# The last down projection of a SwiGLU layer, computed one Strassen product at a time

## The chip, the cores and the metric

The kernel runs on one core of one Trainium2 chip. The metric is the time of one execution on the device in microseconds (us). Of several runs the median is given.

## The reference, cut to what matters

S = 2048 tokens, D = 1024, F = 3584, all in bf16.

```
xn  = layernorm(x)
s   = linear_attention(xn, wqkv, wo)
h   = silu(xn @ w_gate) * (xn @ w_up)        # 2048 x 3584
B   = h @ w_down                             # 2048 x 1024: the down projection
out = x + s * silu(B)
```

## The kernel before, in words

The attention part comes first and writes `s` to a scratch array in HBM (`s_dram`). The feed-forward part follows in two passes of 1024 tokens (`passes`, the upper half of the tokens first). In a pass the gate and up products come as 28 units ("keys": 14 slices of 256 columns, gate and up), and their results make `h`, which stays in SBUF as one tile `hT` of [128, 28, 1024]. Then `emit_down` computes the down projection of the pass.

All these products are done by a seven-product scheme of the Strassen kind (Winograd's form). For the down projection the 1024 tokens of `h` are split into an upper and a lower half (`TB` = 512 tokens each), its 3584 columns into even and odd blocks of 128, and w_down into 2 x 2 blocks. With A for h and B for w_down there are sums S1 = A21 + A22, S2 = S1 - A11, S3 = A11 - A21, S4 = A12 - S2 of h and four sums T1 to T4 of w_down. The latter were formed in the first pass and lie in HBM in packs: `wd_drams[j]` holds for two of the 14 blocks an "a" part (T1, T2, T3, B11) and a "b" part (B21, B22, T4). A product is a sum over 14 blocks, so 14 matmuls of 128x512 for each of the four token tile pairs; with seven products and four pairs there are 392.

`emit_down` goes over the token tile pairs in two halves. Phase a (`step_a`) computes four products at once for one pair, into four PSUM banks: for each block k the products with B11, T2, T3 and T1. Phase b (`step_b`) computes the other three. The sums S1 to S3 of h are made unit by unit by `emit_hs` (L1064 to L1067: four operations on [128, 512], S4 in place of A21) into a ring of six buffers, just ahead of phase a, mostly on VectorE. `evac_a` and `evac_b` add the products up on VectorE and apply the silu on ScalarE. The last pair of the last pass is done by `finish`, product after product, with the last one split into 384 and 128 columns.

`fin` (L1096 to L1098) ends an output block: two operations on VectorE, y * s and + x, and a store on SP's queue. The pieces of x and s for it (`io`) are loaded by `io_load` on the same queue, five to eight ahead, in the order of the list `fq`.

The order on TensorE (PE), VectorE (DVE), ScalarE (ACT) and GpSimd (POOL) is written out by hand (`manual_schedule`); a scheduler places the transfers in SP's queue. Weight buffers come from a ring of eight (`wgu`, 1 MB each), filled in the order of `w_seq` by `load_w_to`. PSUM is held by two pools: `pps` has four tiles of one bank, `ppd` has two tiles of two banks each. The waits between engines are set by the framework, from what each instruction reads and writes.

In the gate and up stage `emit_b` adds a second round of products to the tile `zw` of `ppd`, whose two halves were read by two VectorE operations after the first round:

```python
            nc.vector.scalar_tensor_tensor(out=s3[:], in0=zw[:, 0, :], scalar=rc, in1=s2[:],
                                           op0=ALU.mult, op1=ALU.add)                        # L968
            nc.vector.scalar_tensor_tensor(out=dst, in0=zw[:, 1, :], scalar=rc_of(key),
                                           in1=s3[:], op0=ALU.mult, op1=ALU.add)             # L981
            mb = prod(x_[:], lambda k: w[:, HK + k, 0:P], lambda k: x1[:, HK + k, :], False)
            prod(zw[:, 0, :], lambda k: T4[:, k, :], lambda k: a22[:, k, :], False)
            prod(zw[:, 1, :], lambda k: w[:, HK + k, P:2 * P], lambda k: S4[:, k, :], False)
```

Lines that the text names: L512, L515, L517 and L528 are transposes, copies and products of the first stage of the kernel; L939 is the matmul of the gate and up products; L1006, L1008, L1020 write `h`; L1124 is the matmul of the down projection; L1163 to L1171 and L1183 to L1192 are its evacuation; L234 loads the packs of w_down.

Of the kernel before, what the change touches and what calls it, by code (L numbers as in the profile page):

```python
# [9 lines left out]
ACT = mybir.ActivationFunctionType  # L10
# [11 lines left out]
def kernel(  # L22
# [164 lines left out]
    NPASS = NB // 2  # L187
    passes = list(range(NPASS - 1, -1, -1))
    NWA = NFG // 2
    w_seq = []  # L190
    for p in passes:
        for fg in range(NFG):
            w_seq.append((p, "g", fg))
            w_seq.append((p, "u", fg))
        for kd in ("a", "b"):
            for j in range(NWA):
                w_seq.append((p, kd, j))
# [10 lines left out]
    def wd_q(t):  # L208
        return t[:].rearrange("p h a b -> p (h a b)").rearrange("p (q n) -> p q n", n=D)
# [15 lines left out]
    def load_w():  # L225
        key = w_seq[w_next[0]]
        w_next[0] += 1
        if key in w_tiles:
            return
        p, kind, k = key  # L230
        t = w_slot()
        if kind in ("a", "b"):
            src = wd_drams[k][0 if kind == "a" else 1]
            nc.sync.dma_start(out=t[:].rearrange("p h a b -> p (h a b)")[:, 0:2 * WDN[kind]],  # L234
                              in_=src[:].rearrange("p k q n -> p (k q n)"))
        elif key[1:] in pk_drams:
            gate([nc.sync.dma_start(out=t[:], in_=pk_drams[key[1:]][:])], first_gate[0], sync=True)
        else:
            load_gu(t, kind, k, first_gate[0])
            raw_keys.add(key)  # L240
        w_tiles[key] = t
# [684 lines left out]
    with ExitStack() as p3:  # L926
# [7 lines left out]
        def k2(shape, dt, name):  # L934
            return kp.tile(shape, dt, name=name, tag="k2")
# [117 lines left out]
        def emit_hs(h, hf, m, eng):  # L1053
            r = (NWA * hf + m + 5) % 6
            if r >= 3:
                st = m4.tile([P, HK, TB], F16, name="hs", tag="m4")
            else:
                st = sp.tile([P, HK, TB], F16, name="S%d" % r, tag="S%d" % r)
            sv = st[:].rearrange("p a b -> p (a b)").rearrange("p (q k t) -> p q k t", q=4, k=2)
            hv = h[:, 4 * m:4 * m + 4, :].rearrange("p (k a) t -> p k a t", a=2)  # L1060
            t1, t2 = slice(hf * HT, (hf + 1) * HT), slice(TB + hf * HT, TB + (hf + 1) * HT)
            a11, a12, a21, a22 = hv[:, :, 0, t1], hv[:, :, 1, t1], hv[:, :, 0, t2], hv[:, :, 1, t2]
            S1, S2, S3 = [sv[:, q] for q in range(3)]
            eng.tensor_tensor(out=S1, in0=a21, in1=a22, op=ALU.add)  # L1064
            eng.tensor_tensor(out=S2, in0=S1, in1=a11, op=ALU.subtract)
            eng.tensor_tensor(out=S3, in0=a11, in1=a21, op=ALU.subtract)
            eng.tensor_tensor(out=a21.bitcast(F16), in0=a12, in1=S2, op=ALU.subtract)  # L1067
            s_ring[(hf, m)] = (S1, S2, S3)
# [3 lines left out]

        fq = []
        for p in passes:
            fq += [(p, t + TPB, 1) for t in range(TPB)]
            for hf in (1, 0):
                for t in (2 * hf, 2 * hf + 1):
                    fq += [(p, t + TPB, 0), (p, t, 1), (p, t, 0)]
# [23 lines left out]
        def emit_down(p, h, base, last, more_S, next_S):  # L1102
# [151 lines left out]
            for hf in (1, 0):  # L1254
# [25 lines left out]
                else:  # L1280
                    for f in fins2:
                        f()

        base = 0
        for pi, p in enumerate(passes):
            h = hp.tile([P, FC, TB2], BF16, name="hT", tag="hT")
            keys = [(p, kd, fg) for fg in range(NFG) for kd in ("g", "u")]
            n = len(keys)
            first = pi == 0
            last_pass = pi == NPASS - 1  # L1290

            if first:
                first_gate[0] = marks[("S", NB - 1, 0)]

            def raw(j):
                return 0 <= j < n and keys[j] in raw_keys

            def pipe(j):
                if raw(j):
                    emit_st0(keys[j], w_tiles[keys[j]])  # L1300

            def pipe1(k, i):
                if raw(k):
                    emit_st1(keys[k], grp[keys[i + 1]][4][:, 0:1])

            def pipe2(j):
                if raw(j):
                    t = w_tiles[keys[j]]
                    emit_st2(keys[j], t, later=j == n - 1)
                    emit_lk(keys[j][2])  # L1310
                    if j < n - 1:
                        emit_T(keys[j], t)
                    raw_keys.discard(keys[j])

            wd_live = {}

            def wd_pipe(i):
                if (i - 3) % 3 == 0 and i // 3 - 1 in wd_live:
                    key, t = wd_live[i // 3 - 1]
                    w = raw_view(key, t)  # L1320
                    nc.scalar.activation(out=w, in_=w, func=ACT.Copy, scale=cs_all[:, kcol(key):kcol(key) + 1])
                if (i - 1) % 3 == 0 and (i - 1) // 3 in wd_live:
                    emit_st0(*wd_live[(i - 1) // 3])

            def wd_pipe1(i):
                if (i - 2) % 3 == 0 and (i - 2) // 3 in wd_live:
                    emit_st1(wd_live[(i - 2) // 3][0], grp[keys[i + 1]][4][:, 1:2])

            def wd_pipe2(i):
                m, r = divmod(i + 1, 3)  # L1330
                if r == 1 and m - 1 in wd_live:
                    emit_T(*wd_live[m - 1])
                elif r == 0:
                    if m - 1 in wd_live:
                        emit_st2(*wd_live[m - 1], later=True)
                    if NWE + m < NFG:
                        t = w_slot()
                        load_wd(t, NWE + m)
                        wd_live[m] = ((p, "w", NWE + m), t)

            def more_S(m):
                if first:
                    scale_h(h, 2 * m, nc.scalar)
                    scale_h(h, 2 * m + 1, nc.vector)
                emit_hs(h, 0, m, nc.vector)

            def next_S(m):
                emit_hs(h, 1, m, nc.vector)

            def tail():  # L1350
                emit_hs(h, 0, 2, nc.vector)
                if first:
                    scale_h(h, 7, nc.scalar)
                emit_hs(h, 0, 3, nc.vector)

            na0 = 6 if first else 8
            load_w_to(base + na0)
            if first:
                wd_pipe2(-1)
            emit_a(keys[0])  # L1360
            emit_c22(keys[0])
            first_gate[0] = None
            for i in range(n):
                load_w_to(base + i + (na0 if i < n - 7 else 8 if i > n - 6 or not first else 7))
                if i + 1 < n:
                    emit_a(keys[i + 1])
                    emit_c22(keys[i + 1])
                for j in (range(5) if i == 0 else (i + 4,) if i != n - 6 else ()):
                    pipe(j)
                if first:  # L1370
                    wd_pipe(i)
                    for k in {n - 4: (0,), n - 3: (2, 4), n - 2: (5, 6)}.get(i, ()):
                        scale_h(h, k, nc.scalar)
                mb = emit_b(keys[i])
                if first and i in range(n - 6, n - 1):
                    io_load(mb)
                pipe1(i + (4 if i == n - 5 else 3), i)
                if first:
                    wd_pipe1(i)
                if i == n - 2:  # L1380
                    emit_hs(h, 0, 0, nc.gpsimd)
                if i == n - 1:
                    emit_hs(h, 0, 1, nc.vector)
                emit_evac(keys[i], h, tail if i == n - 1 else None)
                pipe2(i + (4 if i == n - 5 else 3))
                if first:
                    wd_pipe2(i)
                    if i == 5:
                        emit_lk(0)
                    if i == n - 5:  # L1390
                        emit_lam()
                    elif i == n - 4:
                        emit_sc(keys[-1], w_tiles[keys[-1]])
                        emit_T(keys[-1], w_tiles[keys[-1]])
                        scale_h(h, 1, nc.vector)
                    elif i == n - 3:
                        scale_h(h, 3, nc.vector)
                if deferred:
                    deferred.pop(0)()
            base += n  # L1400
            emit_down(p, h, base, last_pass, more_S, next_S)
            base += 2 * NWA
    man.close()

# [30 lines left out]
```

## Time and profile before

| | |
|---|---|
| median of 3 runs | 758.12 us (758.07 to 758.3) |
| span of the profiled execution | 756.7 us |
| what lies outside the span, by the median | 1.4 us |
| PE busy | 746.6 us, 99% of the span |
| DVE busy | 558.5 us, 74% |
| ACT busy | 376.3 us, 50% |
| POOL busy | 278.4 us, 37% |
| down projection of the last pass, first to last matmul | 667.97 to 752.77 us |

The page gives one profiled execution: the span from its first to its last instruction, and the busy time of each engine in it. It gives no other time of that execution; what lies outside is the difference to the median of the timed runs. A matmul's shown duration is longer than the interval to the next, since matmuls are pipelined: 128x512 is shown with 379 ns, and the next starts 216 ns after it.

### The profile page before, as it was taken

The page shows a single profiled execution, that of the slowest core. Times are in us where ns is not written, and L with a number is a line of the kernel's source. Part 1 is how long each engine was busy: PE and PEld are TensorE (multiplying, and loading weights), DVE is VectorE, ACT ScalarE, POOL GpSimd, SP SyncE. Part 2 cuts the span into 40 slices and gives each one's busy share as a digit, 9 for nine tenths or more (in the row PEclk, how much of TensorE's full clock was granted, in tenths as well). Part 3 has the DMA queues.
Part 4 walks back from the last instruction along what each step waited for, and adds up shares of the span by engine and source line. Part 5 has one row for each costly group of instructions (what it writes and reads, how often), then busy time and mean ns, then how long its engine had stood idle before and what let it go on. Part 6 is the DMA issues. An engine that isn't in the chain of part 4 may idle for free.

```text
span 756.7 us, 10426 instructions
## 1 busy us (share of the span) xinstructions
PE 746.6 (99%) x3662; PEld 349.0 (46%) x3731; DVE 558.5 (74%) x1031; ACT 376.3 (50%) x526; POOL 278.4 (37%) x352
## 2 busy tenths in 40 slices
PE   8999999999999999999999999999999999999997
PEld 4544544454454444444444444444444444444443
DVE  6687787896697788888889775368676777787335
ACT  5677776889956565666659311132322223211122
POOL 2444799998540276868585000100000000200000
PEclk9999999999999999999999999999999999999999
DMA  9968799879679668878799236398644445530824
GB/s 316 295 149 146 223 334 300 302 137 307 201 180 298 229 217 292 309 268 312 278 329 408 86 121 239 124 377 321 229 174 167 167 168 173 180 133 15 283 83 135
DMA packets 105845, 170.30 MB, mean 225 GB/s; under 512 B 34816, under 2 KB 82176, under 8 KB 95168
## 3 DMA queue, kind: packets, MB, share of 16 engines
q1 hardware_dynamic: 100144, 144.99, 59.3%
q0 software_dynamic: 4208, 22.15, 7.5%
q10 hardware_dynamic: 1440, 2.49, 0.9%
q8 instruction: 29, 0.48, 0.3%
q14 instruction: 24, 0.20, 0.1%
HBM read 111.67 MB, written 50.59 MB: 214 GB/s over the span
## 4 chain that ended last, share of the span: by engine, by line
PE 97%; DVE 1%; ACT 1%; issue 1%; ACTq 0%; DVEq 0%
PE zw L939 26%; PE kv_ps L528 15%; PE xb L939 13%; PE dzw L1124 12%; PE yb L939 6%; PE q_ps L183 6%; PE dx L1124 6%; PE dy L1124 3%; PE fx L790 3%; PE s_ps L748 2%; PE kvz L550 1%; PE nd L717 1%; PE df L1124 1%; PE warm_ps L564 1%; DVE w_sb L283 0%
## 5 line engine op out<-in xcount | busy, mean ns | idle before, releaser
L939 PEld LDWEIGHTS <-w_sb 128*128 128x128 f16 (+1 forms) x1568 | 152.1, 98 | 182.7
L939 PE MATMUL xb<-xnT,w_sb 128*128 128x512 bf16 x420 | 113.3, 379 | 1.5
L528 PE MATMUL kv_ps<-wkv_sb,xnT 128*128 128x512 bf16 x499 | 112.9, 379 | 1.1 <-DVE xnT L515 0.3
L939 PE MATMUL zw<-xnT,w_sb 128*128 128x512 bf16 x448 | 105.8, 379 | 0.0
L939 PE MATMUL zw<-S,w_sb 128*128 128x512 f16 x448 | 105.8, 379 | 0.0
L295 POOL TENSOR_TENSOR w_sb<-w_sb 128x512 f16<-128x512 bf16 x42 | 50.2, 1195 | 95.7 <-DVE w_sb L283 51.3
L260 ACT ACTIVATE w_sb<-w_sb 128x2048 bf16<-128x2048 bf16 x42 | 79.9, 1902 | 4.4 <-DMA w_sb<-in_B_w_up_dram 4.4
L1124 PE MATMUL dx<-w_sb,hT 128*128 128x512 bf16 x202 | 76.6, 379 | 0.3
L528 PEld LDWEIGHTS <-xnT 128*128 128x128 bf16 x512 | 48.4, 98 | 55.9 <-ACT xnT L517 0.8
L1124 PEld LDWEIGHTS <-hT 128*128 128x128 bf16 (+1 forms) x462 | 44.7, 98 | 52.4
L183 PE MATMUL q_ps<-xnT,wq_sb 128*128 128x512 bf16 x249 | 58.0, 379 | 0.4
L1015 ACT ACTIVATE sg<-cg 128x1024 bf16<-128x1024 f32 x28 | 29.6, 1057 | 57.4 <-DVE cg L1008 57.4
L939 PE MATMUL yb<-S,w_sb 128*128 128x512 f16 x224 | 57.4, 378 | 0.1
L1124 PE MATMUL dzw<-w_sb,hT 128*128 128x512 f16 (+1 forms) x190 | 57.0, 379 | 0.0
L1008 DVE SCALAR_TENSOR_TENSOR cg<-zw,rc_all,s 128x1024 f32<-128x1024 f32 x28 | 35.9, 1284 | 25.5 <-PE zw L939 13.8
L967 DVE SCALAR_TENSOR_TENSOR s<-yb,rc_all,s 128x512 f32<-128x512 f32 x42 | 31.5, 749 | 28.1 <-ACT s L966 28.1
L296 POOL TENSOR_TENSOR w_sb<-w_sb 128x512 f16<-128x512 bf16 x42 | 50.5, 1201 | 3.3
L1064 POOL TENSOR_TENSOR hs<-hT 128x512 f16<-128x512 bf16 x2 | 2.5, 1250 | 132.6 <-ACT sg L1015 132.6
L298 POOL TENSOR_TENSOR w_sb<-w_sb 128x512 f16<-128x512 bf16 x42 | 50.2, 1196 | 0.0
L297 POOL TENSOR_TENSOR w_sb<-w_sb 128x512 f16<-128x512 bf16 x42 | 50.2, 1195 | 0.0
L1098 POOL DMA_DIRECT2D out_dram<-io x16 | 8.7, 542 | 101.9 <-DVE io L1097 101.6
L966 ACT ACTIVATE s<-xb,rcl 128x512 f32<-128x512 f32 x14 | 9.6, 687 | 65.3 <-PE xb L939 65.3
(179 smaller groups left out, 1187.4 us busy)
## 6 DMA issues: line engine op xcount, KB each, us to landing
w_sb<-pk_g SPq DMA_DIRECT2D x27, 1024.0 KB, 6.3
pk_g<-w_sb SPq DMA_DIRECT2D x14, 1024.0 KB, 5.0
w_sb<-wd SPq DMA_DIRECT2D x14, 1024.0 KB, 6.0
w_sb<-pk_u SPq DMA_DIRECT2D x14, 1024.0 KB, 5.0
pk_u<-w_sb POOLq DMA_DIRECT2D x13, 1024.0 KB, 5.3
w_sb<-wd SPq DMA_DIRECT2D x14, 768.0 KB, 4.8
w_sb<-in_B_w_gate_dram SPq DMA_DIRECT2D x14, 512.0 KB, 6.7
w_sb<-in_B_w_down_dram SPq DMA_DIRECT2D x28, 256.0 KB, 4.9
```

The source lines that it names most:

```text
L183: nc.tensor.matmul(q_ps[:], lhsT=wq_sb[:, dc, g * P:(g + 1) * P], rhs=xn_ap(dc, btok), start=(dc == 0), stop=(dc == DC - 1))
L260: nc.scalar.activation(out=junk, in_=raw_view(key, t), func=ACT.Square, accum_out=asum[:])
L295: nc.gpsimd.tensor_tensor(out=T1, in0=b12, in1=b11, op=ALU.subtract)
L296: nc.gpsimd.tensor_tensor(out=T2, in0=b22, in1=T1, op=ALU.subtract)
L297: nc.gpsimd.tensor_tensor(out=T3, in0=b22, in1=b12, op=ALU.subtract)
L298: nc.gpsimd.tensor_tensor(out=T4, in0=b21, in1=T2, op=ALU.subtract)
L528: mm = nc.tensor.matmul(kv_ps[:], lhsT=xn_ap(dc, tok), rhs=wkv_sb[:, dc, c * CW:(c + 1) * CW], start=(dc == 0), stop=(dc == DC - 1))
L939: mm = nc.tensor.matmul(out, lhsT=lhs(k), rhs=rhs(k), start=(first and k == 0), stop=(k == HK - 1), skip_group_check=True)
L967: nc.vector.scalar_tensor_tensor(out=s2[:], in0=y_[:], scalar=rc, in1=s1[:], op0=ALU.mult, op1=ALU.add)
L1008: nc.vector.scalar_tensor_tensor(out=d12, in0=zw[:], scalar=rc, in1=s2[:, None, :].to_broadcast([P, 2, TB]), op0=ALU.mult, op1=ALU.add)
L1015: nc.scalar.activation(out=sg[:, 1:3, :], in_=cf[:], func=ACT.Silu)
L1124: nc.tensor.matmul(out, lhsT=lhs, rhs=rhs, start=first, stop=lastk, skip_group_check=True)
```

## The change

In the last pass `emit_down_m` takes the place of `emit_down`. It goes over the seven products in the order 1, 2, 7, 6, 5, 4, 3 (product 1 is A11 B11, 2 is A12 B21, 3 is S4 B22, 4 is A22 T4, 5, 6 and 7 are S1 T1, S2 T2, S3 T3), and within each over the four token tile pairs (`TPB` = 4), 14 matmuls each. The loads take one product's slice out of all seven packs, in two halves per product, so a half comes as four transfers with rows of 1 KB instead of one with rows of 6 or 8 KB. The sums of h are made for all blocks at once: S3 in two buffers of the pool `xnp`, S1, S2 and S4 in place of A21, A11 and A12. The banks of a product come from `pps` (products 1 and 2, 6, 4) or from `ppd`, two token tiles to one tile (products 7, 5 and 3). Partial sums are kept in `kA` and `kB`. The order of the outputs in `fq` follows. The sums that the last unit of the gate and up stage made ahead (`emit_hs`, `tail`) are left out in the last pass.

```diff
+    M_ORDER = (1, 2, 7, 6, 5, 4, 3)
+    M_PACK = {1: ("a", 3), 5: ("a", 0), 6: ("a", 1), 7: ("a", 2), 2: ("b", 0), 3: ("b", 1), 4: ("b", 2)}
...
+        if p == passes[-1]:
+            w_seq += [(p, "m", (M, hf)) for M in M_ORDER for hf in range(2)]
+            continue
...
+        elif kind == "m":
+            (M, hf), (kd, q) = k, M_PACK[k[0]]
+            v = wd_q(t).rearrange("p q n -> p (q n)").rearrange("p (k n) -> p k n", n=CW)
+            for j in range(NWA):
+                k0, k1 = max(2 * j, NWA * hf), min(2 * j + 2, NWA * (hf + 1))
+                if k0 < k1:
+                    nc.sync.dma_start(out=v[:, k0 - NWA * hf:k1 - NWA * hf],
+                                      in_=wd_drams[j][0 if kd == "a" else 1][:, k0 - 2 * j:k1 - 2 * j, q])
...
+            if p == passes[-1]:
+                fq += [(p, t + dt, cc) for dt, cc in ((0, 0), (TPB, 1), (TPB, 0), (0, 1)) for t in range(TPB)]
+                continue
...
+        def emit_down_m(p, h, base):
+            hv = h[:].rearrange("p (k a) t -> p k a t", a=2)
+            A11, A12 = hv[:, :, 0, 0:TB], hv[:, :, 1, 0:TB]
+            A21, A22 = hv[:, :, 0, TB:TB2], hv[:, :, 1, TB:TB2]
+            S1, S2, S4 = [v.bitcast(F16) for v in (A21, A11, A12)]
+            s3_ = [xnp.tile([P, NWA, TB], F16, name="S3h", tag="xn8") for _ in range(2)]
+            EV = (nc.vector, nc.vector, nc.sync)
...
+            def sums(out, a, b_, op, part=slice(0, NFG)):
+                for k in range(part.start, part.stop, 2):
+                    nc.vector.tensor_tensor(out=out(k), in0=a[:, k:k + 2], in1=b_[:, k:k + 2], op=op)
...
+            def s3_sums():
+                for k in range(NFG):
+                    nc.vector.tensor_tensor(out=S3(k), in0=A11[:, k], in1=A21[:, k], op=ALU.subtract)
...
+            def mm(M, t, k, out, first, cols=slice(0, CW)):
+                nc.tensor.matmul(out, lhsT=lhs_of(M)(k)[:, t * P:(t + 1) * P], rhs=w_of(M, k)[:, cols],
+                                 start=first and k == 0, stop=k == NFG - 1, skip_group_check=True)
+
+            def prod_t(M, t, out, first):
+                for k in range(NFG):
+                    mm(M, t, k, out, first)
+
+            def s_banks():
+                return [pps.tile([P, CW], FP32, name="dx", tag="s")[:] for _ in range(TPB)]
+
+            def d_banks():
+                v = [ppd.tile([P, 2, CW], FP32, name="dz", tag="d") for _ in range(TPB // 2)]
+                return [v[t // 2][:, t % 2] for t in range(TPB)]
...
+            def load(n):
+                load_w_to(base + 2 * n + NPK)
+
+            load(0)
+            E = s_banks()
+            KA = kept("kA")
+            for t0 in (0, 2):
+                for k in range(NFG):
+                    for t in (t0, t0 + 1):
+                        mm(1, t, k, E[t], True)
+                if t0 == 0:
+                    s3_sums()
+                for t in (t0, t0 + 1):
+                    nc.scalar.copy(out=KA[t], in_=E[t])
+            load(1)
+            sums(at(S1), A21, A22, ALU.add)
+            g = []
+            for t in range(TPB):
+                prod_t(2, t, E[t], False)
+                g.append(silu(E[t], "g11"))
+                if t == 0:
+                    sums(at(S2), S1, A11, ALU.subtract)
+                else:
+                    fin(p, t - 1, 0, g[t - 1], *EV)
+            load(2)
+            fin(p, TPB - 1, 0, g[-1], *EV)
+            O = d_banks()
+            KB = kept("kB")
+            for t in range(TPB):
+                prod_t(7, t, O[t], True)
+                add(KB[t], O[t], KA[t])
+                if t == 0:
+                    sums(at(S4), A12, S2, ALU.subtract)
+            load(3)
+            E = s_banks()
+            for t in range(TPB):
+                prod_t(6, t, E[t], True)
+                add(KB[t], E[t], KB[t])
+                add(KA[t], E[t], KA[t])
+            load(4)
+
+            def out_of(M, bank, K, t, row, cc, pre):
+                c = k2([P, CW], FP32, "c%d" % M)[:]
+                add(c, bank, K)
+                g_ = silu(c, "g%d" % M)
+                if pre is not None:
+                    fin(*pre, *EV)
+                return (p, row, cc, g_)
+
+            pre = None
+            O = d_banks()
+            for t in range(TPB):
+                prod_t(5, t, O[t], True)
+                pre = out_of(5, O[t], KB[t], t, t + TPB, 1, pre)
+            add(KA[-1], O[-1], KA[-1])
+            E = s_banks()
+            for t in range(TPB):
+                prod_t(4, t, E[t], True)
+                pre = out_of(4, E[t], KB[t], t, t + TPB, 0, pre)
+            fin(*pre, *EV)
...
+            for t in range(TPB - 1):
+                prod_t(3, t, O[t], False)
+                pre = out_of(3, O[t], KA[t], t, t, 1, pre)
+            fin(*pre, *EV)
...
-            emit_down(p, h, base, last_pass, more_S, next_S)
+            if last_pass:
+                emit_down_m(p, h, base)
+            else:
+                emit_down(p, h, base, last_pass, more_S, next_S)
```

The end of `emit_down_m`, left out here, computes the last tile of product 3 in two banks of `pps`, 384 and 128 columns, as `finish` does it with its last product.

More of the change, by code (lines that the diff above doesn't have):

```diff
@@ L1282, in emit_down, with S3, lhs_of, at @@
                         f()
+        def emit_down_m(p, h, base):
[5 more added lines that the diff above has]
+            EV = (nc.vector, nc.vector, nc.sync)
+            def S3(k):
+                return s3_[k // NWA][:, k % NWA]
+            def lhs_of(M):
+                if M == 7:
+                    return S3
+                v = {1: A11, 2: A12, 3: S4, 4: A22, 5: S1, 6: S2}[M]
+                return lambda k: v[:, k]
+            def sums(out, a, b_, op, part=slice(0, NFG)):
+                for k in range(part.start, part.stop, 2):
+                    nc.vector.tensor_tensor(out=out(k), in0=a[:, k:k + 2], in1=b_[:, k:k + 2], op=op)
+            def at(v):
+                return lambda k: v[:, k:k + 2]
+            def s3_sums():
+                for k in range(NFG):
+                    nc.vector.tensor_tensor(out=S3(k), in0=A11[:, k], in1=A21[:, k], op=ALU.subtract)
+            def w_of(M, k):
+                t = w_tiles[(p, "m", (M, k // NWA))]
+                v = wd_q(t).rearrange("p q n -> p (q n)").rearrange("p (k n) -> p k n", n=CW)[:, k % NWA]
+                return v.bitcast(F16) if M >= 4 else v
+            def mm(M, t, k, out, first, cols=slice(0, CW)):
[9 more added lines that the diff above has]
+                return [v[t // 2][:, t % 2] for t in range(TPB)]
+            def kept(nm):
+                v = [m4.tile([P, 2, CW], FP32, name=nm, tag="m4") for _ in range(TPB // 2)]
+                return [v[t // 2][:, t % 2] for t in range(TPB)]
+            def add(out, a, b_):
+                nc.vector.tensor_tensor(out=out, in0=a, in1=b_, op=ALU.add)
+            def silu(c, nm):
+                g_ = k2([P, CW], BF16, nm)[:]
+                nc.scalar.activation(out=g_, in_=c, func=ACT.Silu, scale=rch)
+                return g_
+            def load(n):
[55 more added lines that the diff above has]
+            fin(*pre, *EV)
+            hs_ = [slice(0, 3 * CW // 4), slice(3 * CW // 4, CW)]
+            ps = [pps.tile([P, CW], FP32, name="df%d" % i, tag="s")[:] for i in range(2)]
+            for i in range(2):
+                nc.scalar.copy(out=ps[i][:, 0:hs_[i].stop - hs_[i].start], in_=KA[-1][:, hs_[i]])
+            pre = None
+            for t in range(TPB - 1):
+                prod_t(3, t, O[t], False)
+                pre = out_of(3, O[t], KA[t], t, t, 1, pre)
+            fin(*pre, *EV)
+            t = TPB - 1
+            g12 = k2([P, CW], BF16, "g12")[:]
+            for i, cs in enumerate(hs_):
+                o_ = ps[i][:, 0:cs.stop - cs.start]
+                for k in range(NFG):
+                    mm(3, t, k, o_, False, cs)
+                nc.scalar.activation(out=g12[:, cs], in_=o_, func=ACT.Silu, scale=rch)
+                fin(p, t, 1, g12, *EV, cols=cs)
@@ L1379 @@
                     wd_pipe1(i)
[L1380 to L1384, printed above, removed]
+                if not last_pass:
+                    if i == n - 2:
+                        emit_hs(h, 0, 0, nc.gpsimd)
+                    if i == n - 1:
+                        emit_hs(h, 0, 1, nc.vector)
+                emit_evac(keys[i], h, tail if i == n - 1 and not last_pass else None)
                 pipe2(i + (4 if i == n - 5 else 3))
```

## The prediction

> **What bounds the kernel now.** I read the page first (busy times, the chain that ended last), then the last 90 us in stretches of 10 us, then TensorE's (PE's) timeline there, and at last the few places early in the kernel where PE really waits for another engine.
>
> ```profile
> PE 746.6 (99%) x3662; PEld 349.0 (46%) x3731; DVE 558.5 (74%) x1031; ACT 376.3 (50%) x526; POOL 278.4 (37%) x352
> PE 97%; DVE 1%; ACT 1%; issue 1%; ACTq 0%; DVEq 0%
> ```
>
> PE is busy for 99% of the span and carries 97% of the chain. So the kernel is one queue of matmuls, and a change can help only by taking matmuls out, by closing a gap, or by shortening what follows the last matmul. It can hurt by opening a gap.
>
> ```profile
> 680.00:690.00 10.00, 9.95 (x48) 4.52 (x47) 5.20 (x11) 1.31 (x2) 0.00 (x0) 1.00 0.01 2
> 690.00:700.00 10.00, 10.00 (x47) 4.56 (x47) 9.41 (x23) 1.31 (x2) 0.00 (x0) 1.00 0.08 26
> 740.00:750.00 10.00, 9.95 (x48) 4.61 (x47) 5.98 (x12) 2.84 (x5) 0.00 (x0) 1.00 0.57 181
> 750.00:757.00 7.00, 2.77 (x27) 1.84 (x24) 3.13 (x9) 1.89 (x4) 0.00 (x0) 0.86 0.19 59
> ```
>
> ```profile
> 667.97 0.38 PE L1124 MATMUL dx<-w_sb,hT 128*128 128x512 bf16 x1
> 743.51 3.18 PE L1124 MATMUL dz<-w_sb,hT 128*128 128x512 f16 x14
> 746.53 6.24 PE L1124 MATMUL df<-w_sb,hT 128*128 128x512 bf16 x41
> ```
>
> First the stretches, whose columns are the length, then busy time of PE, weight load, VectorE (DVE), ScalarE (ACT), GpSimd (POOL), the granted clock, DMA share and GB/s; then PE's timeline. The stage that is changed runs from 667.97 to 752.77 (746.53 + 6.24). Before the last group there are 26 x 14 = 364 full matmuls in 746.53 - 667.97 = 78.56 us, 0.2158 us from start to start: no gap at all. The 14 that go into one bank in a row (dz) take 746.53 - 743.51 = 3.02 us, again 0.216 each, so repeating a bank costs nothing. DVE, not PE, has the slack. Behind the last matmul lie 756.7 - 752.77 = 3.9 us, and outside the span 758.12 - 756.7 = 1.4 us.
>
> **The change, part by part.** In the built order both programs have the same matmuls: seven products x 4 token tiles x 14, with the last one split 384 + 128. PE's work is 84.8 us before and after; nothing is won there.
>
> *Sums of h.* Away go 14 units of four 128x512 sums, 52 on DVE at 0.42 (21.9 us) and 4 on POOL at 1.15. Instead DVE gets 14 of 128x512 (5.9 us) and 21 of 128x1024. A 128x1024 sum of 16-bit data isn't in the trace; the 128x512 form takes 0.425, the 128x1536 form (L1020) 0.954, which puts it at 0.69 on the straight line and at 0.85 as two of the small. I take 0.69 (14.5 us in all) and keep 0.85 for the range. They run beside PE: DVE ends the last piece of h near 671.2; S3 ends near 677, S1 near 682, S2 near 686.5. They are needed at product 7 (692), 5 (716 and later) and 6 (704). The first product needs only A11, whose last piece (L1006) ends at 669.1 and is read as k = 13 at 667.97 + 26 x 0.216 = 673.6. So cost nothing; without that cover DVE would stand 4 to 5 us in PE's way for each sum.
>
> *Weights.* 14 loads become 56 on SP's queue (a product's slice q comes out of seven buffers, in rows of 1 KB). SP needs 0.32 to 0.5 us for an issue, so 8 x 0.43 = 3.4 us for each 12 us product. Queued behind them are the output stores and the x/s pieces for `fin`. The halves of products 1, 2, 7 and the first of 6 are issued in the seven 6 us units before 668, those of 5, 4 and 3 three products ahead of their use. The wqkv loads at the start have 1 KB rows too:
>
> ```profile
> 5.00:10.00 5.00, 4.69 (x28) 2.18 (x26) 3.65 (x11) 1.68 (x5) 0.00 (x0) 1.00 1.09 356
> ```
>
> At 356 GB/s a 0.92 MB half product takes 2.6 us; even at 150 GB/s it takes 6.1 us. Nothing; uncovered it would be that much a half product.
>
> *Evacuation, and here is the cost.* Products 7, 5 and 3 put two token tiles into the two halves of one PSUM tile (`d_banks`: tile t is half t % 2). The halves are different banks, but waits are made by tile. In the built order of the changed kernel the first matmul of the second half waits for the DVE operation that reads the first half. The other turns are hidden: a bank of product 1 is copied by ACT (0.59) 6 us before product 2 adds to it, and DVE's 24 adds of 0.69 and ACT's silus of 0.72 fit beside tiles of 3.0 us. Five are not: product 7, t=1 (for `kB` of t=0) and t=3 (`kB` of t=2); product 5, t=1 and t=3 (`c5`); product 3, t=1 (`c3`). Product 3, t=3 goes to other banks; products 1, 2, 6, 4 have a bank tile each. The kernel before holds the same kind of wait: in `emit_b` the first matmul into zw's first half waits for the operation of L981 that reads the second half. There it is free, as DVE ended it at 664.5 and PE comes at 666.2. In the change nothing lies between: the add can't start before the matmul ahead of it has ended. Behind the waiting matmul all of PE's queue stands. The price of such a turn, PE to DVE to PE, stands in the chain early in the kernel, and the add's in the groups of the last 100 us:
>
> ```profile
> 9.50 0.24 PE tr_ps L512 x4
> 9.74 0.02 issue
> 9.76 0.44 DVE xnT L515
> 10.20 0.05 issue
> 10.24 3.19 PE kv_ps L528 x14
> ...
> L1165 DVE TENSOR_TENSOR kept<-dzw,s 128x512 f32<-128x512 f32 x2 | 1.4, 693 | 0.2
> L1168 DVE TENSOR_TENSOR kept<-dzw,s 128x512 f32<-128x512 f32 x2 | 1.4, 681 | 0.0
> ```
>
> One turn: the last matmul is shown 0.379 long, the next would have started 0.216 after it, so 0.163; hand-over 0.02; add 0.69; hand-over 0.05. Sum 0.92 us. Five: 4.6 us. Bounds: 0.88 (add 0.681, both hand-overs 0.02) and 1.01 (the 0.751 of a scalar_tensor_tensor from PSUM, both 0.05): 4.4 to 5.05.
>
> Can DVE be late for one? For product 7, t=3 the seven S4 sums and `kB` of t=1 go first. `kB` of t=0 ends 3.9 us into the product, that of t=2 may start at 10.16. In those 6.3 us DVE has 7 x 0.69 + 0.69 = 5.5 us to do; at 0.85 it is 6.6, and 0.4 us comes on top. For product 5, t=3 a `fin` goes first (0.85 us, in the 3 us of a tile), with pieces loaded a pass earlier. For product 3, t=1 the last two `fin` of product 4 go first; their pieces are issued some 8 us ahead and land in 2.5. A late piece does stop DVE, which takes its queue in order; once before:
>
> ```profile
> 742.25 0.42 DVE L1096 TENSOR_TENSOR g<-g,io 128x512 bf16<-128x512 bf16 x1 [2.40 <-DMA io<-s_dram]
> ```
>
> *The tail* is the same in kind: 384 + 128 columns, two silus, four products with x and s, two stores. The tile before it leaves an add (0.69), a silu (0.72) and two `fin` in both kernels. 3.9 us stays.
>
> Sum: 758.12 + 4.6 = 762.7 us, against the profiled span 756.7 + 4.6 = 761.3 and the same 1.4 outside.
>
> **The clock.** In the first 12 us PE pauses twice (0.25 us before 7.60, 0.30 before 10.24) and the granted clock stays 1.00:
>
> ```profile
> 7.00:8.00 1.00, 0.75 (x6) 0.29 (x4) 0.96 (x3) 1.00 (x2) 0.00 (x0) 1.00 1.07 367
> ```
>
> By this row a pause costs itself alone. The Trainium skill, TensorE: Matmul & The Clock Gate, section "A second HAM failure mode: psum-queue depth-cycling", speaks against the change: frequent short PE pauses while cycling through banks can make the clock gate swing to half rate. By its window of about 3.4 us ("What's actually happening"), one such window for each pause would add some 1.7 us five times, an estimate of 771 us. No row of this case shows a pause of 0.9 us between two busy stretches.
>
> **The rivals.** *No waiting* (not slower): each half can be filled while the other is read, PE walks on, and the time is 758.1. It takes over where a turn costs under 0.3 us (5 x 0.3 = 1.5). For it: the halves are different banks. Against it: the waits stand in the built order, and the add alone is 0.68. *Feeding fails*: a load or an x/s piece comes late ahead of a `c5` or `c3` add. Price: the 2.40 of the row above once or twice, 765 to 767.5. Against it: 8 us of lead for the pieces, more for the loads. *The clock swings*: at worst all of the 58 us from the first pause on at the 0.86 shown in the last stretch, + 9 us: 772. Against it: 1.00 everywhere that PE has work. *Faster*: the only store of time is the 3.9 us behind the last matmul, and its operations stay; a gain of 1.5 us would need two stores' landings (1.5 to 1.7 each) to shrink to one. That the change does something else than it says is out: matmuls, tiles and stores agree in the built order.
>
> **How the numbers follow.** About 0.2% (1.5 us) can be told from no change. Forecast 0.87; no waiting 0.05; feeding 0.03; clock 0.03; faster 0.02. The forecast's own bounds are 758.12 + 4.4 - 0.1 and 758.12 + 5.05 + 0.4 + 0.2 (the runs before lie -0.05 to +0.2 round the median), 762.4 to 763.8. One turn that doesn't bind takes 0.92 off, and one further wait of about half a microsecond may come on top: 761.6 to 764.3. Slower 0.93, same 0.05, faster 0.02.
>
> **What would show it.** PE's busy time stays at 746 to 747. PE's waits name DVE `kB` (2), `c5` (2) and `c3` (1), each shown as 0.76 (0.92 less the 0.163 that counts as busy). The stage takes 84.8 + 4.6 = 89.4 us from its first to its last matmul. The first gap comes 27 us after the stage's start (two products and a tile: 9 x 14 x 0.216), and the clock stays 1.00. I am wrong if PE shows fewer than four such gaps, if one is over 1.2 us, or if any names a DMA.

## The result, and the profile after

The changed kernel takes 762.90 us (median of 4 runs, 762.65 to 763.09) against 758.21 us before (4 runs, 758.07 to 758.45). The ratio is 1.0061, with a 95% interval of 1.0047 to 1.0076: slower by 4.69 us, where 4.6 were predicted. The profiled execution took 762.88 us itself, with a span of 761.1.

From the page, first the busy times, then the shares in the chain that ended last:

```profile
PE 750.4 (99%) x3731; PEld 348.7 (46%) x3731; DVE 557.4 (73%) x1018; ACT 376.7 (50%) x529; POOL 273.9 (36%) x348
PE 96%; DVE 2%; ACT 1%; DMA 0%; issue 0%; ACTq 0%; DVEq 0%
```

DVE's share of the chain has gone from 1% to 2%, a hint that it now stands in PE's way somewhere. In the totals that is hardly to be seen, as PE is still busy for 99%. The place shows in the stretches (columns: length; busy time of PE, weight load, DVE, ACT and POOL; granted clock; DMA share; GB/s):

```profile
680.00:690.00 10.00, 10.00 (x48) 4.57 (x47) 5.30 (x11) 2.99 (x5) 0.00 (x0) 1.00 0.60 194
690.00:700.00 10.00, 9.22 (x44) 4.10 (x43) 6.38 (x13) 0.69 (x1) 0.00 (x0) 1.00 0.79 242
700.00:710.00 10.00, 9.22 (x44) 4.09 (x43) 2.92 (x6) 0.00 (x0) 0.00 (x0) 1.00 0.49 149
720.00:730.00 10.00, 8.44 (x40) 3.64 (x38) 3.59 (x7) 2.17 (x3) 0.00 (x0) 1.00 0.09 28
740.00:750.00 10.00, 9.22 (x44) 4.11 (x42) 4.44 (x9) 2.73 (x5) 0.00 (x0) 1.00 0.21 70
```

In the stretch from 680 PE has no gap. In those from 690, 700 and 740 0.78 us each are missing, and twice that from 720 to 730, at a granted clock of 1.00 throughout. What PE waited for is told by PE's waits (us in total, times, longest):

```profile
PE dz L1334 <- DVE c L1353: 2.3, 3, 0.8
PE dz L1334 <- DVE kB L1353: 1.6, 2, 0.8
PE warm_ps L577 <- DVE warm L574: 1.5, 1, 1.5
```

L1334 is the matmul of the changed stage, L1353 the add that reads a product from PSUM; `c` stands for `c5` and `c3`. The third line belongs to the start of the kernel. No transfer is among PE's waits in the changed stage. The timeline of PE and DVE there (start, duration, what, and in brackets the idle time before it and who ended it):

```profile
667.70 24.34 PE L1334 MATMUL dx<-w_sb,hT 128*128 128x512 bf16 x112
670.17 4.78 DVE L1326 TENSOR_TENSOR S3h<-hT 128x512 f16<-128x512 bf16 x14
674.87 8.51 DVE L1319 TENSOR_TENSOR hT<-hT 128x1024 f16<-128x1024 bf16 x14
691.88 3.19 PE L1334 MATMUL dz<-w_sb,S3h 128*128 128x512 f16 x14
695.10 0.69 DVE L1353 TENSOR_TENSOR kB<-dz,kA 128x512 f32<-128x512 f32 x1 [1.42 <-PE dz L1334]
695.71 4.29 DVE L1319 TENSOR_TENSOR hT<-hT 128x1024 f16<-128x1024 bf16 x7
695.85 6.20 PE L1334 MATMUL dz<-w_sb,S3h 128*128 128x512 f16 x28 [0.78 <-DVE kB L1353]
699.92 0.68 DVE L1353 TENSOR_TENSOR kB<-dz,kA 128x512 f32<-128x512 f32 x1
702.09 0.69 DVE L1353 TENSOR_TENSOR kB<-dz,kA 128x512 f32<-128x512 f32 x1 [1.48 <-PE dz L1334]
702.83 3.18 PE L1334 MATMUL dz<-w_sb,S3h 128*128 128x512 f16 x14 [0.78 <-DVE kB L1353]
705.85 12.25 PE L1334 MATMUL dx<-w_sb,hT 128*128 128x512 f16 x56
...
721.90 6.20 PE L1334 MATMUL dz<-w_sb,hT 128*128 128x512 f16 x28 [0.78 <-DVE c L1353]
728.89 3.18 PE L1334 MATMUL dz<-w_sb,hT 128*128 128x512 f16 x14 [0.78 <-DVE c L1353]
...
747.96 6.20 PE L1334 MATMUL dz<-w_sb,hT 128*128 128x512 bf16 x28 [0.78 <-DVE c L1353]
754.00 3.22 PE L1334 MATMUL df<-w_sb,hT 128*128 128x384 bf16 x28
```

Up to 705.85 this is product 7 with its two turns. The 14 matmuls of its first tile begin at 691.88. The last of them begins 13 x 0.2157 later, at 694.69, so the next would have begun at 694.90, after one more interval of 0.2157. It begins at 695.85, after the add of 695.10: a pause of 0.95 us, of which 0.78 is shown as idle. The same 0.78 stands before the matmuls at 702.83, and before three more at 721.90, 728.89 and 747.96 (`c`). Five such pauses are 4.75 us. The stage runs from 667.70 to 754.00 + 3.22 = 757.22, that is 89.52 us instead of 84.80.

### The profile page after: what moved, and what is told of

It reads as the page before. It is cut to its first block, busy times and chain, and to the rows that moved or that the text cites. A ratio compares the mean times of both kernels' runs of the same rounds, so it can differ in the third digit from the quotient of the medians.

```text
span 761.1 us, 10540 instructions
## 1 busy us (share of the span) xinstructions
PE 750.4 (99%) x3731; PEld 348.7 (46%) x3731; DVE 557.4 (73%) x1018; ACT 376.7 (50%) x529; POOL 273.9 (36%) x348
## 4 chain that ended last, share of the span: by engine, by line
PE 96%; DVE 2%; ACT 1%; DMA 0%; issue 0%; ACTq 0%; DVEq 0%
PE zw L952 25%; PE kv_ps L541 15%; PE xb L952 13%; PE yb L952 6%; PE q_ps L183 6%; PE dzw L1140 6%; PE dx L1334 6%; PE dz L1334 4%; PE dx L1140 3%; PE fx L803 3%; PE s_ps L761 2%; PE dy L1140 2%; PE kvz L563 1%; PE nd L730 1%; DVE w_sb L296 0%; PE fx L761 0%
## 5 line engine op out<-in xcount | busy, mean ns | idle before, releaser
L952 PE MATMUL xb<-xnT,w_sb 128*128 128x512 bf16 x448 | 115.0, 379 | 0.0
L1334 PEld LDWEIGHTS <-hT 128*128 128x128 f16 (+1 forms) x350 | 33.7, 98 | 42.0 <-issue 3.2
L1334 PE MATMUL dx<-w_sb,hT 128*128 128x512 bf16 (+1 forms) x224 | 48.8, 379 | 0.0
L1140 PE MATMUL dx<-w_sb,hT 128*128 128x512 bf16 x112 | 42.4, 379 | 0.0
L979 ACT ACTIVATE s<-xb,rc_all 128x512 f32<-128x512 f32 x42 | 28.3, 674 | 21.8 <-issue 12.8
```

Source lines behind the costliest of these rows:

```text
L952: mm = nc.tensor.matmul(out, lhsT=lhs(k), rhs=rhs(k), start=(first and k == 0), stop=(k == HK - 1), skip_group_check=True)
L979: nc.scalar.activation(out=s1[:], in_=x_[:], func=ACT.Copy, scale=rc)
L1140: nc.tensor.matmul(out, lhsT=lhs, rhs=rhs, start=first, stop=lastk, skip_group_check=True)
L1334: nc.tensor.matmul(out, lhsT=lhs_of(M)(k)[:, t * P:(t + 1) * P], rhs=w_of(M, k)[:, cols], start=first and k == 0, stop=k == NFG - 1, skip_ ...
```

## The experiments

The theory: PE waits because the two halves of a `d_banks` tile share their waits; all of the loss is five turns, and the rest of the change costs nothing. Its rivals: the narrow loads or the in-place sums cost a part of the 4.7 us; a bank cannot be read while the next one is filled; a turn has a fixed price, whatever DVE has to do; the pauses also lower PE's clock. Each edit below is made to the changed kernel. The first four ran beside the same runs of the kernel before (15 runs, median 758.24 us), the last two beside others (7 runs, median 758.31).

**Neighbouring tiles in different PSUM tiles (e1_alternate).**

```diff
             def d_banks():
                 v = [ppd.tile([P, 2, CW], FP32, name="dz", tag="d") for _ in range(TPB // 2)]
-                return [v[t // 2][:, t % 2] for t in range(TPB)]
+                return [v[t % 2][:, t // 2] for t in range(TPB)]
```

> The banks of products 7, 5 and 3 are dealt out so that neighbouring token tiles lie in different PSUM tiles (t % 2 picks the tile, t // 2 the half); all else as in the changed kernel. Shared-tile theory: each wait now reaches back to the add of the token tile before last, which DVE ended 2 us or more earlier, so all five pauses go. PE's waits name no kB or c5 or c3, the stage takes 84.8 us from first to last matmul, and the time is 762.9 - 5 x 0.95 = 758.15 us, the time of the kernel before within 0.3. Rival, the rest of the change has a price or a gain of its own (1 KB rows, sums in place, the other order of outputs), which the pauses cover: the time then lies off 758.2 by more than 0.5 us. Rival, a bank cannot be read while the next one is filled: the pauses stay, 762.9 us.

Measured: 758.33 us (11 runs, 757.75 to 759.16), ratio 1.0001 (0.9993 to 1.0010). The timeline of PE in this kernel:

```profile
667.91 24.34 PE L1334 MATMUL dx<-w_sb,hT 128*128 128x512 bf16 x110
692.09 12.25 PE L1334 MATMUL dz<-w_sb,S3h 128*128 128x512 f16 x56
...
740.43 9.23 PE L1334 MATMUL dz<-w_sb,hT 128*128 128x512 bf16 x41
749.50 3.22 PE L1334 MATMUL df<-w_sb,hT 128*128 128x384 bf16 x28
```

Each product now is one unbroken group, with no bracket behind it; the stage takes 749.50 + 3.22 - 667.91 = 84.81 us, as before the change. The banks, the matmuls, the adds, the loads with 1 KB rows, the sums in place and the order of the outputs are those of the changed kernel; only which halves share a tile is different. So the whole loss comes from the pairing, and the rest of the change is worth nothing that these runs can tell, in either direction (by the interval, between -0.5 and +0.8 us). Each bank is read here while the next token tile's is filled, so the reading itself doesn't ask for the pause.

**Product 7 alone in four one-bank tiles (e2_product7_apart).**

```diff
             fin(p, TPB - 1, 0, g[-1], *EV)
-            O = d_banks()
+            O = s_banks()
             KB = kept("kB")
```

> Product 7 alone takes four PSUM tiles of one bank each, token tiles in the same order; products 5 and 3 stay in the two-bank tiles. Shared-tile theory: two of the five pauses go, three of 0.95 us stay: 762.9 - 1.9 = 761.0 us, PE's waits name c three times and kB not at all. Rival, the pauses come from DVE being behind in its queue: those of product 5 and 3 would change too as product 7 runs 1.9 us shorter, and the time would not be 761.0 within 0.4.

Measured: 760.97 us (5 runs, 760.67 to 761.14), ratio 1.0035 (1.0021 to 1.0049). Of the changed stage PE's waits keep one line:

```profile
PE dz L1334 <- DVE c L1353: 2.3, 3, 0.8
```

The two turns on `kB` are gone, the three on `c` stay, and 760.97 - 758.24 = 2.73 us is 0.91 for each of them. The loss counts by turns.

**Product 6 too with two token tiles to one PSUM tile (e3_product6_shared).** Product 6 has two adds behind each tile (`kB`, then `kA`), and both read the bank.

```diff
             load(3)
-            E = s_banks()
+            E = d_banks()
             for t in range(TPB):
                 prod_t(6, t, E[t], True)
```

> Product 6 is put into the two-bank tiles as well; its banks are read by two DVE adds one after the other. Shared-tile theory: two pauses come on top, for t=1 and t=3 of product 6, and each lasts until the second add has ended: 0.163 + 0.03 + 0.61 (start to start of the two adds) + 0.68 + 0.06 = 1.55 us, 1.38 us of it shown as PE's wait for kA. Time 762.9 + 3.1 = 766.0 us. Rival, a pause has a price of its own whatever DVE does: 762.9 + 1.9 = 764.8 us.

Measured: 765.92 us (4 runs, 765.86 to 766.09), ratio 1.0102 (1.0088 to 1.0115). PE's waits:

```profile
PE dz L1334 <- DVE kA L1353: 2.8, 2, 1.4
PE dz L1334 <- DVE c L1353: 2.3, 3, 0.8
PE dz L1334 <- DVE kB L1353: 1.6, 2, 0.8
```

Two turns are added, each shown as 1.4 where one add gave 0.8. The time rises by 765.92 - 762.90 = 3.02 us, 1.51 for each. So a turn has no fixed price: PE waits for everything that DVE has to do with that bank.

**The S4 sums ahead of the add (e5_s4_first).** DVE takes its queue in order, so seven sums that PE doesn't wait for, ahead of an add that it does wait for, should lengthen one pause to over 3.5 us. That is also long enough to ask what a pause does to the clock.

```diff
             for t in range(TPB):
                 prod_t(7, t, O[t], True)
-                add(KB[t], O[t], KA[t])
                 if t == 0:
                     sums(at(S4), A12, S2, ALU.subtract)
+                add(KB[t], O[t], KA[t])
```

> In product 7 the seven S4 sums are put ahead of the add of the first token tile in DVE's queue; nothing else differs. Shared-tile theory: the wait of the second token tile's first matmul reaches through DVE's queue. The sums start when the last output of product 2 is done (693.7) and take 4.3 us, then the add 0.69, so PE stands from 694.9 to 698.65, 3.75 us (3.58 shown) in place of 0.95, and the other four pauses stay: 762.9 + 2.8 = 765.7 us. The granted clock stays 1.00. Rival, the clock gate: the Trainium skill, TensorE: Matmul & The Clock Gate, section What's actually happening, has the clock fall to half after an idle window of some 3.4 us. A window at half clock after this pause would be seen as matmul starts 0.43 us apart and would add 1.7 us: 767.4 us.

Measured: 767.27 us (4 runs, 767.04 to 767.38), ratio 1.0119 (1.0105 to 1.0133). The timeline, then the stretches around the pause:

```profile
693.55 4.30 DVE L1319 TENSOR_TENSOR hT<-hT 128x1024 f16<-128x1024 bf16 x7
697.77 0.69 DVE L1353 TENSOR_TENSOR kB<-dz,kA 128x512 f32<-128x512 f32 x1
698.51 7.89 PE L1334 MATMUL dz<-w_sb,S3h 128*128 128x512 f16 x28 [3.49 <-DVE kB L1353]
```

```profile
695.00:699.00 4.00, 0.51 (x4) 0.25 (x3) 3.45 (x6) 0.00 (x0) 0.00 (x0) 1.00 0.92 287
699.00:700.00 1.00, 1.00 (x5) 0.34 (x4) 0.00 (x0) 0.00 (x0) 0.00 (x0) 0.61 0.85 277
700.00:701.00 1.00, 1.00 (x4) 0.39 (x3) 0.00 (x0) 0.00 (x0) 0.00 (x0) 0.50 0.70 245
701.00:702.00 1.00, 1.00 (x3) 0.30 (x2) 0.00 (x0) 0.00 (x0) 0.00 (x0) 0.50 0.06 21
702.00:703.00 1.00, 1.00 (x5) 0.40 (x4) 0.00 (x0) 0.00 (x0) 0.00 (x0) 0.69 0.00 0
703.00:704.00 1.00, 1.00 (x6) 0.49 (x5) 0.59 (x1) 0.00 (x0) 0.00 (x0) 1.00 0.75 244
```

Two prices are to be read here. The pause is 3.49 + 0.16 = 3.65 us instead of 0.95; that explains 762.90 + 2.7 = 765.6 and no more, where 765.7 were expected with an unchanged clock. What came is close to the 767.4 of the rival. The other 1.7 us stand in the matmuls after the pause: 28 of them take 7.89 us, where they took 6.20. PE is busy in each of these stretches, with a clock of 0.61, 0.50, 0.50 and 0.69: half speed for 0.78 + 1 + 1 + 0.62 = 3.4 us, which loses 1.7. The clock is still 1.00 up to 699.22 (1.00 less the 0.78 us of the second stretch), 0.7 us after the pause, and falls only then.

**Four of the seven ahead (e6_s4_four_first), and six (e7_s4_six_first).** Where between 0.95 and 3.65 us does a pause begin to lower the clock?

```diff
                 prod_t(7, t, O[t], True)
+                if t == 0:
+                    sums(at(S4), A12, S2, ALU.subtract, slice(0, 8))
                 add(KB[t], O[t], KA[t])
                 if t == 0:
-                    sums(at(S4), A12, S2, ALU.subtract)
+                    sums(at(S4), A12, S2, ALU.subtract, slice(8, NFG))
```

With six ahead, the bound between the two parts is 12 in place of 8.

> Four of the seven S4 sums stand ahead of the first token tile's add of product 7, three behind it. By the queue: four sums take 2.45 us from 693.6, the add ends at 696.65, PE stands 1.85 us in place of 0.95 and the other four pauses stay: 762.9 + 0.9 = 763.8 us if the clock stays 1.00, as it did after pauses of 0.95 and 1.55. If a pause of half a clock window is enough to lower it: about 1.7 us more, 765.5 us.

> Six of the seven S4 sums stand ahead of the first token tile's add of product 7. By the queue: the add ends at 697.8, PE stands 3.05 us: 762.9 + 2.1 = 765.0 us if the clock stays 1.00, 766.7 us with one window of 3.4 us at half clock, as after the pause of 3.66 us. A window that runs freely and has to be idle as a whole would leave the clock alone, since the pause is shorter than the window; a window that only has to be mostly idle would lower it in part of the runs or in all.

Measured with four ahead: 763.66 us (4 runs, 763.51 to 764.19), ratio 1.0072 (1.0057 to 1.0087). Its timeline:

```profile
697.20 6.20 PE L1334 MATMUL dz<-w_sb,S3h 128*128 128x512 f16 x28 [1.68 <-DVE kB L1353]
```

A pause of 1.68 + 0.16 = 1.84 us, and the 28 matmuls after it take 6.20 us: full clock. This pause costs itself alone, as expected.

Measured with six ahead: 765.01, 765.05, 766.46 and 766.81 us, ratio 1.0095 (1.0078 to 1.0112). These are two groups, one at each of the two expected times, so the median of 765.75 describes no run. Two runs have a mean granted clock of 1.000 and 0.999, the others of 0.998 and 0.997. The profile is that of the 766.81:

```profile
698.12 7.89 PE L1334 MATMUL dz<-w_sb,S3h 128*128 128x512 f16 x28 [2.88 <-DVE kB L1353]
```

A pause of 2.88 + 0.16 = 3.04 us was followed by the same 7.89 us as in e5_s4_first. So a pause of 3.0 us lowered the clock in two of four runs (by their times and mean clocks; one of them was profiled), one of 3.65 us did it every time, and those of 0.95, 1.5 and 1.84 us did not. Where between 1.84 and 3.04 us it begins was not measured.

## Why the prediction was right

*PE's work is the same, and nothing is won.* Shown by e1_alternate: with the pairing undone the stage takes 84.81 us, where it took 84.80 before the change.

*Five turns.* All five were where the order of the waits had put them, two on `kB`, two on `c5` and one on `c3`, the first 694.90 - 667.70 = 27.2 us into the stage (27 predicted). The price of one was made of 0.163 for the matmul's end, 0.02, an add of 0.69, and 0.05; the first pause has 0.16, 0.03, 0.69 and 0.06. So 0.95 us in place of 0.92, five times 0.03 too low; the upper bound of 1.01 held. e2 and e3 confirm the form of this term and not its sum alone: two turns fewer, and two turns with a second add in them, come out at the time that it gives.

*Sums of h.* The unknown price of a 128x1024 sum, taken as 0.69 with 0.85 as bound, is 8.51 / 14 = 0.61 us, and the 128x512 ones come every 4.78 / 14 = 0.34 us and not every 0.42. Both were too high, without effect on the time, as these sums lie beside PE. Their size mattered at one place only, the second `kB` turn: DVE was through with S4 and the `kB` add before it at 700.60, and the next add could begin at 702.09. The 0.4 us kept for this in the range were not needed, by 1.5 us. e5_s4_first is what the same sums cost without that cover. (The lower end of the range is 762.4 - 0.92 = 761.5 by its own terms, not 761.6; nothing hangs on it.)

*Weights and the pieces of x and s.* Costed at nothing, and nothing is what they cost: PE waits for no transfer in the stage, and e1_alternate, with the same loads, takes 758.33. So the rival of a failing feed did not come about. What it would cost with its cover gone was not tried. Of the five turns the least cover was ahead of the `c3` add at 747.22, where two `fin` go first: DVE was through with them only 0.60 us before.

*The tail.* From the last matmul's end at 757.22 to the end of the span at 761.1 are 3.9 us, as before.

*The rival without waiting* described a kernel that could have been written: e1_alternate is this kernel, at 758.33 where the rival had 758.1. Its argument, that the halves are different banks, is true of the banks. The waits, though, are set for each tile, and it is these that PE obeys.

*The clock.* The forecast of 1.00 held for all of the five pauses (1.00 in every stretch with one), and in the experiments for pauses up to 1.84 us. The row of before on which it stood can't carry it, though. This is the chain there, from which the prediction shows the next lines:

```profile
3.80 2.56 PE warm_ps L564 x6
...
7.60 1.90 PE kv_ps L528 x8
```

Both are matmuls of 128x512. The six take 2.56 / 6 = 0.43 us each, as the matmuls at 0.50 in e5_s4_first do, although the views of the first 7 us show a clock of 1.00; the eight come every (1.90 - 0.163) / 8 = 0.22 us. So the pause before 7.60 lies between half and full rate, and only the one of 0.30 us before 10.24 says anything on what a pause costs. For a pause of 0.9 us no row stood, as the prediction says itself: that it costs itself alone was a guess that came true, and the changed kernel is what shows it. The price of the clock's rival was misread as well: the 0.86 of the last stretch is the mean of 1.00 up to about 755.0 and of 0.50 behind it, while PE's last matmul ends at 752.77. No matmul ran at 0.86.

The rival's mechanism exists nevertheless: in these runs it came with one long pause, and not with several short ones. The Trainium skill, TensorE: Matmul & The Clock Gate, has both rules that the prediction set against itself. Its section "A second HAM failure mode: psum-queue depth-cycling" (frequent short pauses between groups of matmuls make the clock swing) is not borne out here by five pauses of 0.95 us in 53 us, nor by seven in e3. What "What's actually happening" says, half rate after an idle window of about 3.4 us, agrees with the fall after 3.65 us in e5_s4_first; but 3.04 us of pause were enough in two of four runs, so the figure is no safe limit for a pause. Of the two alternatives in the expectation of e7, a window that has to be idle as a whole would have left the clock alone; what is left is one that has to be mostly idle. e5_s4_first agrees with it: if the window that decided was as long as the stretch at half rate, 3.4 us, and lay just ahead of it, PE ran matmuls in its last 0.7 us. What sets the two groups of e7 apart was not shown.

*Two side numbers were wrong.* PE's busy time was to stay at 746 to 747 and is 750.4. Two things add to it: the five ends of 0.163 us that now stand free ahead of a pause (0.8), and the number of matmul records. The page of before has 3662, that of after all 3731, and a missing record inside an unbroken row shows as a hole of two intervals less one shown duration, 0.431 - 0.379 = 0.05 us; 69 of them are up to 3.6 us. e1_alternate, with 3666 records and no pause, shows 746.2; e3_product6_shared, with as many records and seven pauses, 747.2, that is 1.0 more for seven ends of 0.163. So a busy time near 99% is no measure of a change of half a per cent here; the gaps by tile are. The other is "the same 1.4 outside" the span: that was one execution's span set against the median of other runs. In the execution profiled after, its own time and span differ by 762.88 - 761.1 = 1.8 us, and in a run of the kernel before, beside the experiments, by 758.33 - 756.5 = 1.8. The spans therefore differ by 4.4 and the medians by 4.69, and it is the stage, longer by 4.72, that agrees with the medians.

No kernel here is faster than the one before. e1_alternate equals it, with a gapless PE, and what is left of this stage is the 3.9 us behind the last matmul, which nothing here touches.

## What to carry to other kernels

Where waits are made by tile, a PSUM tile of two banks is one resource, even if each bank is filled and read by itself: give neighbouring iterations different tiles, or PE and its reader take turns. Such a turn costs the matmul's end, two hand-overs, and everything that the reader's queue holds up to the last operation on that tile, here 0.16 + 0.09 + 0.69 us with one add and 1.5 us with two. It is worth working out for each turn how long the pause gets: up to 1.84 us it cost itself here, at 3.04 us the clock added 1.7 us on top in two runs of four, and at 3.65 us in all four.

## What was not expected of the hardware

- After one long pause PE's clock stayed at 1.00 for 0.7 us (from 698.51 to about 699.2), then was 0.50 for 3.4 us though PE was busy, and then 1.00 again. The 3.04 us pause did this in some runs and not in others, with the same program.
- Sums of 16-bit data in a row on DVE run closer together than their shown durations: 0.34 us from start to start for 128x512 (shown with 0.42 when alone) and 0.61 for 128x1024 (shown with 0.68, in e7_s4_six_first). The timeline of before had this already: there a sum begins 0.34 us after the one ahead of it, at 667.23 and 667.57, and 0.45 where it reads that one's result, at 666.78 and 667.23.
